# Output projections in column tiles that each run over all heads

## The chip, the cores and the metric

The kernel runs on one core of one Trainium2 chip. The metric is the device time of one execution in microseconds (us). Three runs of the kernel before took 823.28 to 824.87 us, with a median of 824.17 us.

## The reference

```
# A: attention over segments of 32 tokens with 8 recurrent memory tokens
xs_all = layernorm(x)                          # [2048, 512]
mem = mem0                                     # [8, 512]
for s in range(64):
    h = concat([mem, xs_all[32*s : 32*s+32]])  # 40 tokens
    q, k, v = h @ Wq, h @ Wk, h @ Wv           # 32 heads of 128
    scores = mask(q @ k.T * 128**-0.5)         # memory rows see all, token rows are causal
    o = softmax(scores) @ v
    o = sum over heads and e of o[t, h, e] * Wo[h, e, :]   # [40, 512]
    mem = o[:8]
    outs.append(o[8:])
h = x + concat(outs)
# B: a channel MLP
y = layernorm(layernorm(h))
out = h + gelu(y @ w1 + b1) @ w2 + b2
```

The inputs are bfloat16. The memory makes the segments a chain: a segment's first products need the first 8 rows of the output projection of the segment before. The change concerns the line with `Wo`.

## The kernel before

**Tiles and stages.** All four weight matrices stay in on-chip memory. Phase one is a loop over 64 segments; four segments make a block of 128 tokens. After it the MLP runs over four groups of 512 tokens. Tokens of a segment are held transposed in `hT` (feature by token, a ring of segments). A segment's 32 columns of `hT` are 24 token columns and 8 memory columns; the 8 remaining tokens of each segment are held in `hB`, one set for a block of four segments, and go through the projections a block ahead ("mixed-in" work, the parts named F).

**Column tiles.** Nearly all matmuls of phase one use TensorE in four column tiles of 32: a weight load puts 32 columns (the 32 tokens) into tile j, a matmul streams up to 512 columns of a weight matrix past it, and its 32 output rows land in partitions 32j to 32j+31 of a PSUM bank. Four matmuls, one for each tile, make a round and run at once.

**The order of work.** A small planner (`Sched`) records every operation with its reads and writes, and then lays out each engine's instruction stream. The order on TensorE is written out by hand (`ORDERS`, one for each position of a segment in its group of four): passes for Q, K and V, the memory scores SC0 and SC1, the products PV0, PV1 and PVA, the output projection WO, the self-attention scores SA, with the parts F0 and F1 in between. Other engines are placed by due times in a segment (`PLAN`). Parts F belong to the next block's Q, K and V in three of four segments; in the fourth (segment number 3 modulo 4), F1 is `wo_B`, the output projection of a block's mixed-in tokens.

**Instruction blocks.** TensorE's instructions are counted in blocks of 256 (`FETCH_N`). `align` counts each operation's instructions (`ni`) and inserts idle weight loads ("pads") into passes, at most 8 each, so that a segment's first instruction stands at a fixed place in its block (`PHASE`, by segment modulo 4). `windows` places DMA transfers from 1.0 us behind one block boundary to 0.8 us ahead of the next; `pauses` lets a few instructions behind a boundary wait for an earlier one of TensorE.

**The output projection.** `wo_units` (L1160 to L1173) makes eight units of eight matmuls, each 32 tokens by 256 columns over one head. Tiles 0 and 1 take half of the heads, tiles 2 and 3 the other half; of a pair, one takes the even 32-column groups of the output, the other the odd ones. So the sums over heads come in two halves, in the upper and the lower 64 partitions. In `wo` (L1178), VectorE transposes the 128x256 result in squares of 32 into `TT` (L1182), which makes it feature by token, and adds the halves (`halves_add`, L1176): first the 8 memory columns into the next segment's `hT`, by two additions of 64 partitions each, then the 24 token columns into `opT`, by two more. In three of four segments that second pair is kept back (`held`, `now`, `late`) and placed in the following segment, behind its softmax.

**The mixed-in projection.** `wo_B` (L1205) makes eight units of four matmuls with 512 columns. Each tile takes 8 of the 32 heads and all output columns, so four partial sums arise. VectorE transposes 128x512 into `TTB` (L1213). GpSimd folds them: `chunk` makes 7 operations for each half (L1222 to L1226), and `fold` spreads the 14 over the tails of three segments, each waiting for the one before.

**Behind it.** `nat` (L1238) turns `opT` back to rows by a DMA transpose, adds the residual, takes the layernorm's statistics in two halves of 256 columns (`half`, `close`; the second is kept back a segment) and stores the rows for the MLP.

Of the kernel before, what the change touches and what calls it, by code (L numbers as in the profile page):

```python
# [24 lines left out]
PHASE = (0, 64, 128, 192)  # L25
# [62 lines left out]
        "opA": (17.5, 10.96, 18.73, 17.5),  # L88
# [533 lines left out]
def build_kernel(nc, A_x, A_mem0, A_Wq, A_Wk, A_Wv, A_Wo, B_w1, B_b1, B_w2, B_b2, out):  # L622
# [3 lines left out]
    with st:  # L626
# [48 lines left out]
        TT = sb("TT", [P, 2, DC, 2, 32], F32)  # L675
        TTB = sb("TTB", [P, DC, 4, 32], F32)
        TTS = sb("TTS", [64, 2, 4, 32], F32)
# [4 lines left out]
        st2 = sb("st2", [P, 2, 2, 6], F32)  # L682
# [116 lines left out]
        turned, held, late, now = [], [], [], []  # L799
# [357 lines left out]
        def wo_cols(h, dh):  # L1157
            return WO[:, h, :].rearrange("p (b two e) -> p two b e", two=2, e=32)[:, dh]

        def wo_units(lhs, reads, bank):  # L1160

            for q in range(8):
                def f(e, q=q):
                    for k in (2 * q, 2 * q + 1):
                        for a in range(2):

                            h = (k // 8) * 16 + 8 * a + k % 8
                            for b in range(2):
                                j = 2 * a + b
                                ins = e.matmul(ps[bank][32 * j:32 * j + 32, 0:256], lhs(slot(h)), wo_cols(h, b), start=(k == 0), stop=(k == 15),  # L1170
                                               tile_position=(0, 32 * j), skip_group_check=True)
                    return ins
                S.op("pe", f, reads=[("WO", q, a) for a in range(2)] + reads(q // 4), writes=[("ps", bank)], dur=0.223, mode=MC, ni=16)  # L1173

        def halves_add(tt, q2, out, cols):
            return lambda e: e.tensor_tensor(out, tt[0:64, :, q2, cols], tt[64:128, :, q2, cols], ALU.add)  # L1176

        def wo(s, bank, mem=True, xrows=True):  # L1178
# [3 lines left out]
            S.op("dve", lambda e: e.transpose(tt.rearrange("p c q t -> p (c q t)"), ps[bank][:, 0:256]), reads=[("ps", bank)], writes=[("TT", par)], dur=t_dve(256) + 0.02)  # L1182
            if mem:
                sl = (s + 1) % RING
                S.op("dve", lambda e: [halves_add(tt, q2, hT[64 * q2:64 * q2 + 64, sl, :, NA:SEG], slice(NA, SEG))(e) for q2 in range(2)][1],
                     reads=[("TT", par)], writes=[("hTm", sl)], dur=0.4)
            if xrows:
                sx = s - 2
                o = opT[:, (sx // 4) % 2, :, 32 * (sx % 4):32 * (sx % 4) + NA]
                tag = S.tag  # L1190

                def rows(after=()):
                    was, S.tag = S.tag, tag
                    o_ = S.op("dve", lambda e: [halves_add(tt, q2, o[64 * q2:64 * q2 + 64], slice(0, NA))(e) for q2 in range(2)][1],
                         reads=[("TT", par)], writes=[("opA", (sx // 4) % 2, sx % 4)], dur=0.53, after=after)
                    S.tag = was
                    return o_
                if s % 4 == 2 and 1 < s // 4 < NTB - 3:
                    held.append(rows)
                elif s % 4 in (3, 0) and 3 < s < NS - 2:  # L1200
                    now.append(rows)
                else:
                    rows()

        def wo_B(bk, bank):  # L1205
            for q in range(8):
                def f(e, q=q):
                    for j in range(4):
                        ins = e.matmul(ps[bank][32 * j:32 * j + 32, :], OTB[:, bk % 2, slot(8 * j + q), :], WO[:, 8 * j + q, :], start=(q == 0), stop=(q == 7),  # L1209
                                       tile_position=(0, 32 * j), skip_group_check=True)  # L1210
                    return ins
                S.op("pe", f, reads=[("WO", g, a) for g in range(8) for a in range(2)] + [("OTB", bk % 2, sg) for sg in range(4)], writes=[("ps", bank)], dur=0.2135, mode=MC, ni=8)
            S.op("dve", lambda e: e.transpose(TTB[:].rearrange("p c q t -> p (c q t)"), ps[bank][:, :]), reads=[("ps", bank)], writes=["TTB"], dur=t_dve(512) + 0.02)  # L1213
            o = opT[:, bk % 2, :, :].rearrange("p c (s t) -> p c s t", s=4)[:, :, :, NA:SEG]

            def chunk(c):
                t = TTB[:, c:c + 2]

                def sums(q):
                    def f(e):  # L1220
                        x, y = [v[0:32, :, q].rearrange("p c (s t) -> p c s t", s=4) for v in (t, TTS)]
                        return e.tensor_tensor(o[32 * q:32 * q + 32, c:c + 2], x, y, ALU.add)  # L1222
                    return lambda after: S.op("pool", f, reads=["TTB", "TTS"], writes=[("opB", bk % 2)], dur=0.31, after=after)
                return [lambda after: S.op("pool", lambda e: e.tensor_copy(TTS[0:64], t[64:128]), reads=["TTB"], writes=["TTS"], dur=0.4, after=after),
# [6 lines left out]
        def fold(n, after=()):  # L1231
            tag, S.tag = S.tag, None
            for f in folds[:n]:
                S.narrow(f(after))
# [154 lines left out]
        for s in range(NS):  # L1389
# [7 lines left out]
            while held:  # L1397
                held.pop()()
# [288 lines left out]
```

## Time and profile before

| | |
|---|---|
| median of three runs | 824.17 us |
| profiled execution, its time | 821.98 us |
| its span, from the first to the last instruction | 820.2 us |
| granted TensorE clock, mean | 0.998 |
| WO matmuls (L1170) | 4224, 144.3 us busy |
| `wo_B` matmuls (L1209) | 512, 44.4 us busy |
| VectorE: transposes into `TT` and `TTB` | 29.1 and 11.3 us |
| VectorE: halves added into `hT` and `opT` | 24.7 and 33.5 us |
| GpSimd: folding (L1222 to L1226) | 40.3, 23.1, 12.6 and 12.4 us |

Busy times are those of one profiled execution. PE is TensorE's matmuls, PEld its weight loads, which overlap them; DVE is VectorE, ACT ScalarE, POOL GpSimd, SP the engine that issues most DMA transfers. The end of a matmul in the records is modelled and lies behind the start of the next one, so the time that a piece of work takes on TensorE is read from start to start. "issue" names idle time in which an engine waited for nothing that the profile shows.

### The profile page before, as it was taken

How to read it: one execution, taken by the hardware profiler on the slowest of the kernel's cores; microseconds unless marked ns; L12 is line 12 of the kernel's file. 1: busy time of each engine (PE TensorE's matmuls, PEld its weight loads, DVE VectorE, ACT ScalarE, POOL GpSimd, SP SyncE). 2: the span in 40 equal slices, each digit the busy share in tenths (PEclk: the TensorE clock that was granted, in tenths of full speed). 3: DMA queues.
4: the chain of work that ended last, by engine and by line, in shares of the span. 5: the costliest groups of instructions: out<-in, count | busy, mean ns of one | idle time of the engine just before them, and what ended most of it. 6: DMA issues, size and time to landing. Idle time of an engine off the chain costs nothing.

```text
span 820.2 us, 43608 instructions
## 1 busy us (share of the span) xinstructions
PE 783.0 (95%) x19317; PEld 425.6 (52%) x18878; DVE 620.3 (76%) x2022; ACT 534.5 (65%) x1512; POOL 350.3 (43%) x886
## 2 busy tenths in 40 slices
PE   3788999999999999999999999999999999999998
PEld 1355555555555555555555555555556555544443
DVE  3367898888888888888888888888889887833211
ACT  1546776767676767676777676767676768833442
POOL 5023333545454545454545444545463534267200
PEclk9999999999999999999999999999999999999999
DMA  8950010101011010101010101010112130265200
GB/s 341 390 174 12 4 33 7 33 27 29 29 27 33 20 39 17 42 13 45 10 43 10 48 11 49 11 48 3 50 29 61 40 96 17 75 165 137 72 26 26
DMA packets 65449, 48.03 MB, mean 59 GB/s; under 512 B 29028, under 2 KB 61676, under 8 KB 65260
## 3 DMA queue, kind: packets, MB, share of 16 engines
q1 hardware_dynamic: 64928, 44.98, 18.6%
q8 instruction: 150, 2.46, 1.3%
q14 instruction: 39, 0.32, 0.1%
q10 hardware_dynamic: 332, 0.27, 0.1%
HBM read 31.08 MB, written 8.13 MB: 48 GB/s over the span
## 4 chain that ended last, share of the span: by engine, by line
PE 74%; DVE 10%; ACT 8%; SPq 5%; issue 1%; DMA 1%; POOL 0%; DVEq 0%; POOLq 0%
PE ps L871 33%; PE ps L1170 14%; PE quad L1576 6%; PE ps L604 5%; PE ps L1569 4%; ACT EC L1053 4%; ACT kq L889 3%; PE quad L1074 3%; DVE PC L1061 3%; SPq L791 3%; DVE KALL L912 2%; SPq L774 2%; PE ps L1209 2%; PE ps L1104 2%; DVE nmc L1044 2%; PE quad L1142 1%
## 5 line engine op out<-in xcount | busy, mean ns | idle before, releaser
L871 PE MATMUL ps<-WQ,hT 128*32 128x512 bf16 x2048 | 157.9, 380 | 6.0 <-DVE hT L1176 5.5
L1170 PE MATMUL ps<-WO,OT 128*32 128x256 bf16 x4224 | 144.3, 275 | 1.3 <-issue 0.6
L871 PE MATMUL ps<-WV,hT 128*32 128x512 bf16 x1780 | 142.9, 379 | 0.0
L890 ACT ACTIVATE kq<-ps 128x512 bf16<-128x512 f32 x160 | 95.6, 598 | 62.1 <-PE ps L871 61.8
L1125 POOL TENSOR_TENSOR PA<-SA,rsa 128x256 bf16<-128x256 f32 x64 | 39.8, 621 | 189.3 <-DVE rsa L1118 176.8
L889 ACT CAST kq<-ps 128x512 bf16<-128x512 f32 x160 | 93.3, 583 | 36.6 <-PE ps L871 36.6
L1170 PEld LDWEIGHTS ps<-WO,OT 128*32 128x32 bf16 x4224 | 96.8, 96 | 26.6 <-ACT OT L889 5.2
L1131 POOL COPY BD<-PTA 32x192 bf16<-32x192 bf16 x256 | 96.1, 376 | 16.7 <-DVE PTA L1127 0.9
L871 PE MATMUL ps<-WK,hT 128*32 128x512 bf16 x1292 | 93.4, 379 | 0.0
L1061 DVE SCALAR_TENSOR_TENSOR PC<-EC,rsc,even 128x128 bf16<-128x128 f32 x256 | 87.9, 368 | 4.4
L871 PEld LDWEIGHTS ps<-WQ,hT 128*32 128x32 bf16 x2048 | 59.8, 96 | 59.9 <-issue 19.2
L912 DVE STREAM_TRANSPOSE KALL<-kq 128x256 f32<-128x256 f32 x160 | 70.5, 441 | 21.3 <-ACT kq L889 19.1
L1053 ACT ACTIVATE EC<-quad,nmc 128x64 f32<-128x64 f32 x252 | 77.2, 312 | 7.8 <-DVE nmc L1044 1.2
L604 PE MATMUL ps<-WK,hT 128*32 128x512 bf16 x756 | 75.7, 379 | 0.6 <-ACT kq L890 0.6
L889 ACT CAST VS<-ps 128x512 bf16<-128x512 f32 x126 | 73.8, 586 | 0.9
L871 PEld LDWEIGHTS ps<-WV,hT 128*32 128x32 bf16 x1780 | 52.0, 96 | 34.2 <-issue 2.0
L912 DVE STREAM_TRANSPOSE QT<-kq 128x256 f32<-128x256 f32 x128 | 56.8, 444 | 15.7 <-ACT kq L890 15.5
L889 ACT CAST OT<-quad 128x128 bf16<-128x128 f32 (+1 forms) x179 | 59.6, 348 | 11.4 <-PE quad L1079 8.3
L1572 ACT ACTIVATE WQ<-ps,b1t 128x512 bf16<-128x512 f32 x42 | 28.9, 688 | 51.9 <-PE ps L1569 51.9
L1116 ACT ACTIVATE SA<-SA 128x256 f32<-128x256 f32 x64 | 26.7, 417 | 55.1 <-DVE SA L1115 52.5
L871 PEld LDWEIGHTS ps<-WK,hT 128*32 128x32 bf16 x1292 | 38.1, 97 | 45.5 <-issue 20.3
L1222 POOL TENSOR_TENSOR opT<-TTB,TTS 32x64 bf16<-32x64 f32 x128 | 40.3, 315 | 33.2 <-DVE opT L1176 24.0
(160 smaller groups left out, 1487.6 us busy)
## 6 DMA issues: line engine op xcount, KB each, us to landing
WV<-in_A_Wv_dram SPq DMA_DIRECT2D x4, 1024.0 KB, 10.4
WK<-in_A_Wk_dram SPq DMA_DIRECT2D x4, 1024.0 KB, 18.0
WQ<-in_A_Wq_dram SPq DMA_DIRECT2D x4, 1024.0 KB, 19.1
WO<-in_A_Wo_dram SPq DMA_DIRECT2D x16, 256.0 KB, 7.5
v_last<-VSB SPq DMA_DIRECT2D x60, 64.0 KB, 3.2
VBD<-v_last SPq DMA_DIRECT2D x60, 64.0 KB, 2.8
h_mid<-xr SPq DMA_DIRECT2D x16, 128.0 KB, 1.8
WQ<-h_mid SPq DMA_DIRECT2D x4, 512.0 KB, 4.4
```

What stands on the lines that cost most here:

```text
L604: return e.add_instruction(mybir.InstMatmult(name="I-%d" % (4000000 + _kept[0]), engine=mybir.EngineType.PE, start_tensor_calc=start, stop ...
L871: ins = e.matmul(o, l, m, start=(k == 0), stop=(k == DC - 1), tile_position=(0, 32 * j), skip_group_check=True)
L889: return {"act": (lambda e: e.copy(out, src), t_act(n, ps_)), "dve": (lambda e: e.tensor_copy(out, src), 0.155 + 1.0e-3 * n * fast)}
L890: return {"act": (lambda e: e.mul(out, src, scale_), t_act(n, ps_)), "dve": (lambda e: e.tensor_scalar(out, src, scale_, None, ALU.mult), ...
L912: S.op("dve", lambda e: e.transpose(out, src), reads=[("kq", i)], writes=[key], dur=t_dve(256) + 0.02)
L1053: return e.activation(EC[:, r, sl, :], o[:, sl, :], ACTF.Exp, bias=nmc[:, r, sl:sl + 1], accum_out=smc[:, r, sl:sl + 1])
L1061: S.op("dve", lambda e, sl=sl, xc=xc: e.scalar_tensor_tensor(PC[:, r, :, :, sl], xc, rsc[:, r, sl:sl + 1], ev, ALU.mult, ALU.mult), reads= ...
L1125: S.either({k: ((lambda e: e.tensor_tensor(PA[:].rearrange("p a t b -> p a b t"), SA[:].rearrange("p (a b) t -> p a b t", b=2), bc2, ALU.m ...
L1131: S.narrow(S.op("pool", lambda e, j=j, rows=rows: e.tensor_copy(BD[rows, par, :, j, :, :], PTA[rows, :, 0:NA, :]), reads=["PTA"], writes=[ ...
L1170: ins = e.matmul(ps[bank][32 * j:32 * j + 32, 0:256], lhs(slot(h)), wo_cols(h, b), start=(k == 0), stop=(k == 15), tile_position=(0, 32 * ...
L1222: return e.tensor_tensor(o[32 * q:32 * q + 32, c:c + 2], x, y, ALU.add)
L1576: S.op("pe", lambda e: e.matmul(quad[:, t, :], gT_of(k, fc)[:, t * P:(t + 1) * P], W2[:, fc, :], start=(fc == 0), stop=(fc == FC - 1)), re ...
```

## The change

Each column tile j now takes the output columns 128c + 32j to 128c + 32j + 31 (c = 0 to 3) over all 32 heads, so that a projection is 128 matmuls of 128 columns, with a weight load each, and every sum is complete. The transposed result is 128x128 and needs plain copies instead of additions. `wo_B` uses the same units, and GpSimd's folding is gone. The copies into `opT` are no longer kept back; the statistics of `nat` are taken in one piece, and `nat` and the loads of x are issued a segment earlier. `PHASE`, the due times of `opA`, and the planner's durations are set anew.

```
-PHASE = (0, 64, 128, 192)
+PHASE = (216, 152, 152, 88)
...
-        "opA": (17.5, 10.96, 18.73, 17.5),
+        "opA": (19.07, 10.96, 10.96, 12.13),
...
-        def wo_cols(h, dh):
-            return WO[:, h, :].rearrange("p (b two e) -> p two b e", two=2, e=32)[:, dh]
+        def wo_cols(h, j):
+            return WO[:, h, :].rearrange("p (c j e) -> p j c e", j=4, e=32)[:, j]
...
             for q in range(8):
                 def f(e, q=q):
-                    for k in (2 * q, 2 * q + 1):
-                        for a in range(2):
-
-                            h = (k // 8) * 16 + 8 * a + k % 8
-                            for b in range(2):
-                                j = 2 * a + b
-                                ins = e.matmul(ps[bank][32 * j:32 * j + 32, 0:256], lhs(slot(h)), wo_cols(h, b), start=(k == 0), stop=(k == 15),
-                                               tile_position=(0, 32 * j), skip_group_check=True)
+                    for n in range(4):
+                        h = (q // 4) * 16 + 8 * (n // 2) + 2 * (q % 4) + n % 2
+                        for j in range(4):
+                            ins = e.matmul(ps[bank][32 * j:32 * j + 32, 0:P], lhs(slot(h)), wo_cols(h, j), start=(q == 0 and n == 0), stop=(q == 7 and n == 3),
+                                           tile_position=(0, 32 * j), skip_group_check=True)
                     return ins
-                S.op("pe", f, ..., dur=0.223, mode=MC, ni=16)
+                S.op("pe", f, ..., dur=0.2315, mode=MC, ni=32)
...
-            S.op("dve", lambda e: e.transpose(tt.rearrange("p c q t -> p (c q t)"), ps[bank][:, 0:256]), ...)
+            S.op("dve", lambda e: e.transpose(tt.rearrange("p c t -> p (c t)"), ps[bank][:, 0:P]), ...)
             if mem:
-                S.op("dve", lambda e: [halves_add(tt, q2, hT[64 * q2:64 * q2 + 64, sl, :, NA:SEG], slice(NA, SEG))(e) for q2 in range(2)][1], ...)
+                S.op("dve", lambda e: e.tensor_copy(hT[:, sl, :, NA:SEG], tt[:, :, NA:SEG]), ...)
             if xrows:
-                def rows(after=()): ...      # two halves_add into opT; held, now or at once
+                S.op("dve", lambda e: e.tensor_copy(o, tt[:, :, 0:NA]), ...)
...
         def wo_B(bk, bank):
-            for q in range(8): ...           # 4 matmuls of 512 columns, 8 heads for each tile
-            S.op("dve", lambda e: e.transpose(TTB[:].rearrange("p c q t -> p (c q t)"), ps[bank][:, :]), ...)
-            folds.extend(chunk(0) + chunk(2))
+            wo_units(lambda sl: OTB[:, bk % 2, sl, :], lambda r: [("OTB", bk % 2, sg) for sg in range(4)], bank)
+            S.op("dve", lambda e: e.transpose(TTB[:].rearrange("p c t -> p (c t)"), ps[bank][:, 0:P]), ...)
+            S.op("dve", lambda e: e.tensor_copy(o, TTB[:].rearrange("p c (s t) -> p c s t", s=4)), ...)
...
-            half(0)                          # bn_stats of 256 columns; close() does the second half later
+            S.op("dve", lambda e: e.bn_stats(st2[:, i, :], xs), ...)
...
-            if sg == 1 and 0 < bk and bk + 4 < NTB:
+            if sg == 0 and 0 < bk and bk + 4 < NTB:
                 load_x(bk + 4)
-            if sg == (3 if bk < NTB - 3 else 2) and bk > 1:
+            if sg == 2 and bk > 1:
                 nat(bk - 2)
```

More of the change, by code (lines that the diff above doesn't have):

```diff
@@ L797, in qbf @@
             return quad[:].bitcast(BF16)[:, :, 2 * c0:2 * c0 + P]
-        turned, held, late, now = [], [], [], []
+        turned = []
         def ln1(tb, after=()):
@@ L1198, in wo @@
[L1198 to L1203, printed above, removed]
-        def wo_B(bk, bank):
[L1206 to L1213, printed above, removed]
-            o = opT[:, bk % 2, :, :].rearrange("p c (s t) -> p c s t", s=4)[:, :, :, NA:SEG]
[L1216 to L1224, printed above, removed]
-                        lambda after: S.op("pool", lambda e: e.tensor_tensor(t[0:64], t[0:64], TTS[0:64], ALU.add), reads=["TTB", "TTS"], writes=["TTB"], dur=0.73, after=after),
-                        lambda after: S.op("pool", lambda e: e.tensor_copy(TTS[0:32], t[32:64]), reads=["TTB"], writes=["TTS"], dur=0.41, after=after)] + [sums(q) for q in range(4)]
-            folds.extend(chunk(0) + chunk(2))
```

62 lines of the change are left out of this document (15 added, 47 removed).

## The prediction

> **What bounds the kernel now.** I read the page first, for the engines' shares, the queues and the chain.
>
> ```profile
> span 820.2 us, 43608 instructions
> PE 783.0 (95%) x19317; PEld 425.6 (52%) x18878; DVE 620.3 (76%) x2022; ACT 534.5 (65%) x1512; POOL 350.3 (43%) x886
> ...
> q8 instruction: 150, 2.46, 1.3%
> ...
> PE 74%; DVE 10%; ACT 8%; SPq 5%; issue 1%; DMA 1%; POOL 0%; DVEq 0%; POOLq 0%
> ```
>
> TensorE is busy 95% and carries the chain, so GpSimd's 43% and VectorE's 76% are cover: relieving them pays only where TensorE waits for them. The row that I rest most on is the third (packets, MB, share of the DMA engines). TensorE's own instructions arrive in 150 packets: 2.46 MB / 150 is 16.4 KB each, and (19317 + 18878) / 150 is 255 instructions, so one packet is a block of 256 matmuls and weight loads (with a few separate waits). The change adds instructions to this queue and to nothing else. So I asked next, in the timeline of TensorE, what happens where a block ends. This is the second half of segment 20; columns are start, duration, engine, line, names, count:
>
> ```profile
> 256.92 0.41 PE L871 MATMUL ps<-WV,hT 128*32 128x512 bf16 x4
> 257.35 0.27 PE L1074 MATMUL quad<-PTC,VS 64*128 64x32 bf16 x8
> 257.46 0.23 PE L1079 MATMUL quad<-PTC,VBD 64*128 64x128 bf16 x2
> 257.66 0.38 PE L1142 MATMUL quad<-BD,VS 64*128 64x48 bf16 x16
> 257.97 0.40 PE L871 MATMUL ps<-WK,hB 128*32 128x512 bf16 x4
> 258.20 0.61 PE L1170 MATMUL ps<-WO,OT 128*32 128x256 bf16 x16
> 258.74 0.27 PE L1074 MATMUL quad<-PTC,VS 64*128 64x32 bf16 x8
> 258.85 0.22 PE L1079 MATMUL quad<-PTC,VBD 64*128 64x128 bf16 x2
> 259.00 1.53 PE L1170 MATMUL ps<-WO,OT 128*32 128x256 bf16 x48
> 260.35 0.39 PE L871 MATMUL ps<-WK,hB 128*32 128x512 bf16 x4
> 260.57 0.69 PE L1104 MATMUL ps<-KALL,QT 128*32 128x32 bf16 x32
> 261.08 0.83 PE L871 MATMUL ps<-WK,hB 128*32 128x512 bf16 x12
> ```
>
> The same self-attention scores (L1104, called SA in the code) in segment 24, and the weight loads of SA in segment 20:
>
> ```profile
> 302.53 0.42 PE L1104 MATMUL ps<-KALL,QT 128*32 128x32 bf16 x32
> 302.78 0.84 PE L871 MATMUL ps<-WK,hB 128*32 128x512 bf16 x12
> ```
>
> ```profile
> 260.36 0.36 PEld L1104 LDWEIGHTS ps<-KALL,QT 128*32 128x32 bf16 x13
> 260.96 0.19 PEld L1104 LDWEIGHTS ps<-KALL,QT 128*32 128x32 bf16 x19 [0.24 <-issue]
> ```
>
> SA took 0.51 us there (260.57 to 261.08) against 0.25 (302.53 to 302.78). The loads stop after 13 of 32 and nothing is waited for but "issue". By the code's count (`align`) a block of segment 20 begins two instructions into the V pass at 256.92 and ends inside SA. The rows agree: ahead of SA stand 4+8+2+16+4+16+8+2+48+4 = 112 matmuls, 224 instructions with their loads, 13 pairs of SA make 250, and the separate waits the rest. So TensorE stopped exactly where a block ended, 3.7 us after it began. The first segment shows it in the output projection itself:
>
> ```profile
> 58.73 1.38 PE L1170 MATMUL ps<-WO,OT 128*32 128x256 bf16 x42
> 60.70 0.40 PE L1170 MATMUL ps<-WO,OT 128*32 128x256 bf16 x6 [0.60 <-issue]
> ```
>
> 42 of 48 matmuls, then idle on "issue" at the next block's first instruction. I conclude that the next block is asked for when the present one is entered, and that a block run through faster than some time T stops TensorE until T is over. How often now, in the list of waits (us, times, longest):
>
> ```profile
> PEld L869 <- DVE hT L1176: 22.4, 48, 1.0
> PE ps L871 <- DVE hT L1176: 5.5, 7, 1.1
> PEld ps L1170 <- ACT OT L889: 5.2, 23, 0.3
> PEld ps L1104 <- issue: 2.2, 8, 0.4
> ```
>
> Eight stalls ahead of SA's loads; by the code's count one segment in four, fifteen in all, has a block that ends in SA when it is 3.7 us old. The kernel sits on the edge of T.
>
> **T, and its bounds.** The stalled SA had its block at about 3.7 + 0.3 = 4.0 us; the unstalled ones had it by 3.7. If eight of fifteen took 4.0 and the other seven as little as 2.5, the mean is 3.3; if those took 3.7, 3.9. Below, no row excludes a smaller T, since a fetch that is not late leaves no row; I keep 2.8 as the low end (one in which seven of fifteen needed 1.4). I take T = 3.3, the low side, because the code keeps its own transfers away from the first 1.0 us after a block boundary (`windows`), and short blocks leave no room for one behind it that could delay the fetch.
>
> **The change, part by part.** *Instructions.* An output projection goes from 64 to 128 matmuls, each with its load: +128 instructions in each of 66. The mixed-in projection `wo_B` goes from 32 to 128 matmuls: +192 in each of 16. So 4x128 + 192 = 704 more per four segments, and `PHASE` says the same: the segments' starting places 0, 64, 128, 192 close after 9 blocks of 256, the new ones 216, 152, 152, 88 after 12 (with some 64 idle loads as padding).
>
> *Where the blocks end.* Counted in instructions from a segment's start, the new layout has the first two projection units at 330 to 394, the second PV at 394 to 414, the six other units to 606, then SA to 670. Boundaries lie at 256k minus the segment's phase. Times between them come from the rows of segment 20 (two units 0.54, PV 0.26, six units 1.35):
> - phase 216: at 40, 296 (in PVA, L1142) and 552 (fifth of the six units): 257.7 to 259.0 + 4.3 x 0.225 = 2.3 us;
> - phase 152, twice: at 104, 360 (end of the first unit) and 616 (in SA): 0.27 + 0.26 + 1.35 + 0.05, about 2.0 us each;
> - phase 88, where the passes between are `wo_B` units of 32 instructions: at 168, 424 (start of the projection), 680 (sixth of six) and 40 of the next segment: about 2.8, 0.54 + 0.26 + 5.4 x 0.225 = 2.0, and 2.7 us.
>
> The six other blocks of a group hold mostly passes of 8 instructions in 0.215 us and last 4.1 to 5.3 us. The six short ones together last 13.8 us and would need 6T: at T = 3.3 that is 19.8, so 6.0 us lost per four segments. Segments 4 to 63 are 15 groups: **+90 us**. At T = 2.8 the block of 2.8 drops out, 5 x 2.8 - 11.0 = 3.0, +45; at 3.85, 9.3 and +140. The opening segments and the tail, with half as many such blocks: +4 (2 to 6).
>
> *The matmuls themselves.* Rounds of four column tiles, from starts: 16 matmuls of 64 columns with 16 loads took 0.12 us, 0.030 a round; twelve rounds of 256 columns 1.35, 0.112.
>
> ```profile
> 401.49 0.30 PE L1036 MATMUL quad<-KALL,ZC 128*32 128x64 bf16 x16
> 401.61 0.39 PE L871 MATMUL ps<-WV,hT 128*32 128x512 bf16 x4
> ```
>
> Between them 128 columns take 0.057: 32 x 0.057 = 1.83 against 16 x 0.112 = 1.79 for a projection, 1.83 against 8 x 0.215 = 1.72 for `wo_B`. 66 x 0.04 + 16 x 0.11 = 4.4, taken as **+5** (0, if columns alone count, to 8).
>
> The Trainium skill, "TensorE: Matmul & The Clock Gate", section "LDWEIGHTS (loading the stationary operand)", speaks against the change: a load takes its columns / 1.2 ns, 27 ns for 32 columns, 107 ns for a round's four against some 55 of matmul. The 0.030 us round above holds four such loads, so this trace disagrees unless the four column tiles load at once.
>
> *The memory chain.* After the projection VectorE transposes, adds halves twice, and only then can the next segment's first pass load hT.
>
> ```profile
> L1182 DVE STREAM_TRANSPOSE TT<-ps 128x256 f32<-128x256 f32 x66 | 29.1, 440 | 26.9 <-PE ps L1170 26.8
> L1176 DVE TENSOR_TENSOR hT<-TT 64x32 bf16<-64x32 f32 x126 | 24.7, 196 | 3.0
> L1063 DVE STREAM_TRANSPOSE PTC<-PC 128x128 f32<-128x128 f32 x128 | 39.9, 311 | 4.4
> L1176 DVE TENSOR_TENSOR opT<-TT 64x96 bf16<-64x96 f32 x128 | 33.5, 262 | 2.9
> L1222 POOL TENSOR_TENSOR opT<-TTB,TTS 32x64 bf16<-32x64 f32 x128 | 40.3, 315 | 33.2 <-DVE opT L1176 24.0
> L1225 POOL TENSOR_TENSOR TTB<-TTB,TTS 64x256 f32<-64x256 f32 x32 | 23.1, 721 | 15.7 <-DVE PC L1061 14.0
> ```
>
> 440 + 2 x 196 = 832 ns becomes 311 (the 128x128 transpose) plus one copy of about 190: 0.33 us shorter. What that was worth:
>
> ```profile
> 408.39 0.41 PE L871 MATMUL ps<-WQ,hT 128*32 128x512 bf16 x4
> ...
> 417.98 0.84 PE L1209 MATMUL ps<-WO,OTB 128*32 128x512 bf16 x12
> 418.85 0.41 PE L871 MATMUL ps<-WQ,hT 128*32 128x512 bf16 x4
> ```
>
> Three rounds of 0.215 end at 418.63, the pass starts at 418.85: 0.22 us lost in a segment of 10.46. Over 63 segments that is 14 at most; the 48 waits of weight loads for hT (22.4 us, in the list above) are mostly hidden behind running matmuls, so I take 7. The 2.2 us of SA stalls and some of the 5.2 for OT fall under the new stalls too. Together **-12** (-5 to -16).
>
> *The rest costs nothing on the path.* The row copies (two adds of 262 ns become one), the smaller transpose in `wo_B`, and GpSimd's folding (40.3 + 23.1 us and the copies beside them) lie on engines with idle time. `nat` (a DMA transpose, then a 128 KB store) and `load_x` (a 128 KB load) move a segment earlier in SP's queue, past that segment's other transfers; none of TensorE's waits listed above is for SP. Undivided statistics hold VectorE about 0.26 us longer at a stretch, 16 times: 4 us if none of it were covered, and the stops of TensorE now cover it.
>
> **Sum**, against the profiled execution: 821.98 + 90 + 4 + 5 - 12 = 909. The median of the runs stands 0.27% above the profiled one, so **911**.
>
> **Rivals.** *A: blocks are never late, and the gains stand.* Then 822 + 5 - 12 + (the OT waits that stay) 3 = 818, with the median's 0.27% 820, a gain of 0.5%. For it: at 3.7 us only half of the SA stalled. Against it: two stops exactly at a block's end, one in the projection. It decides if T is below about 2.0. The Trainium skill, "Runtime: NRT & Kernel Launch", section "Instruction fetch mechanics", gives PE room for 2048 instructions, which would make every block early, and says in the same place that the next page is fetched while the current one runs; the stops bear out the second. I give A 0.11, and 0.03 that small stops (T near 2.1) and gains cancel to within 0.2%, which is about what a measurement of this kernel can tell from no change.
>
> *B: weight loads bound the projection*, one after another. With 0.0275 us per load, the most that hides under today's 0.11 us round of four, a round takes 0.11 instead of 0.057: 32 x 0.053 x 82 = +139, on top of A less its 5, some 954, without any idle "issue" row. SA's and L1036's rows, with loads in 0.008 us each, are against it: 0.02. By the 27 ns of the page of the Trainium skill named above it would be 950.
>
> *C: T is small but not harmless*, 2.1 to 2.8: 826 to 866. For it: the low end above is not excluded. 0.14.
>
> My forecast, T between 2.8 and 3.9, has the rest, 0.70; by itself it spans 860 to 966. Range 826 to 966: the low end takes in C, so that A, the balance near zero and B stay out (0.16), the high end is T = 3.85 with the dear ends of the small terms. Faster 0.11, same 0.03, slower 0.86.
>
> **What would show it.** Queue q8 has about 197 packets, and PE x25,077. Rows L1170's successor and L1104 gain idle "<-issue" of about 1 to 1.5 us, in all four kinds of segment, at the places above; segments last about 11.5 to 13 us, the one with `wo_B` longest. The wait of L871 for hT vanishes. A projection whose matmuls run 1.8 us without an "issue" gap, with hT's wait gone, would prove me wrong and A right; even slow rounds without gaps, B.

## The result: slower by 12.8%, and the profile after

| | before | after |
|---|---|---|
| median of the runs | 823.72 us (822.25 to 824.87, 4 runs) | 928.92 us (926.93 to 930.52, 4 runs) |
| profiled execution, time and span | 821.98 and 820.2 us | 927.4 and 925.7 us |
| granted TensorE clock, mean | 0.998 | 0.996 |

The ratio is 1.128, with a 95% interval from 1.124 to 1.131. The clock is the same, so the 105 us are not a slower TensorE.

The page of after, with the lines that answer to the first ones shown of before (span, engines, the queue of TensorE's instructions, the chain), and its groups of the projection and of the self-attention scores (SA):

```profile
span 925.7 us, 55633 instructions
PE 794.1 (86%) x25068; PEld 469.3 (51%) x25558; DVE 571.7 (62%) x1912; ACT 528.1 (57%) x1497; POOL 261.7 (28%) x662
...
q8 instruction: 199, 3.26, 1.5%
...
PE 70%; issue 11%; ACT 8%; DVE 6%; DMA 2%; SPq 2%; POOL 0%; DVEq 0%
...
L1166 PE MATMUL ps<-WO,OT 128*32 128x128 bf16 x8448 | 152.7, 221 | 42.6 <-issue 38.9
...
L1103 PE MATMUL ps<-KALL,QT 128*32 128x32 bf16 x2048 | 31.4, 178 | 41.7 <-issue 41.7
```

Every engine but TensorE has less to do: VectorE is down from 620.3 to 571.7 us, GpSimd from 350.3 to 261.7. TensorE is busy 11 us more, at 86% instead of 95%, and the chain has 11% "issue", where it had 1%: 11% of 925.7 is 102 us. Almost all of the loss is TensorE standing still and waiting for nothing that the profile shows. The list of waits (us, times, longest) says where:

```profile
PE ps L1103 <- issue: 41.7, 32, 2.0
PE ps L1166 <- issue: 38.9, 34, 2.1
PE ps L870 <- issue: 15.9, 17, 3.2
```

41.7 + 38.9 + 15.9 = 96.5 us. The waits for hT are nearly gone: of the 22.4 us for which TensorE's loads waited for it before, 5.6 are left, in two rows:

```profile
PEld ps L870 <- DVE hT L1178: 4.6, 14, 0.3
...
PEld L868 <- DVE hT L1178: 1.0, 2, 0.5
```

Where the stops stand, in TensorE's timeline: all stops on "issue" from segment 15's end to segment 19's, and one row (277.50) in which a wait is put down to ScalarE.

```profile
232.61 0.34 PE L1166 MATMUL ps<-WO,OT 128*32 128x128 bf16 x10 [1.77 <-issue]
...
236.07 0.40 PE L870 MATMUL ps<-WQ,hT 128*32 128x512 bf16 x4 [0.69 <-issue]
...
245.04 0.57 PE L1166 MATMUL ps<-WO,OT 128*32 128x128 bf16 x28 [1.16 <-issue]
...
257.06 0.35 PE L1103 MATMUL ps<-KALL,QT 128*32 128x32 bf16 x26 [1.07 <-issue]
...
268.97 0.34 PE L1103 MATMUL ps<-KALL,QT 128*32 128x32 bf16 x26 [1.48 <-issue]
...
277.50 0.63 PE L1166 MATMUL ps<-WO,OT 128*32 128x128 bf16 x32 [0.33 <-ACT OT L888]
...
280.96 0.34 PE L1166 MATMUL ps<-WO,OT 128*32 128x128 bf16 x10 [1.23 <-issue]
```

These are the boundaries of the prediction: ahead of the last pass of Q0 and in the fifth of six projection units (phase 216), in SA (phase 152, twice), at the start of the projection and in its sixth unit (phase 88). The resumed rows hold what is left of the pass: 26 of SA's 32 matmuls. TensorE's records show the blocks exactly: each of these rows begins 256 records, or 512 or 768, behind another. So does the row at 277.50. In 14 groups, TensorE began there between 0.36 us ahead of the end of ScalarE's operation and 0.69 us behind it, so that operation isn't what releases it: this is the sixth stop, 0.4 us in the mean.

The fetches themselves are in the trace too, as packets of q8. From 254 to 260 us, around the stop of 257.06, they are the only two transfers (busy tenths of the DMA engines in 40 slices of 0.15 us, and the queue's packets):

```profile
DMA  0000400000000000000000000004000000000000
...
q8 instruction: 2, 0.03, 2.2%
```

The block that ends in this stop was entered at 253.80, 256 records ahead of the resume. The next block's packet starts at 254.75 and takes 0.96 us; TensorE resumes 1.35 us after it has landed. From 80 to 770 us every block has exactly one such packet. In the mean of the six stopped places (14 groups), it starts 1.04 us behind the block's first instruction and takes 1.11 us, and TensorE goes on 1.38 us after its end: 3.53 us from a block's first instruction to the next one's. A block that TensorE runs through in less time ends in a stop.

And the projection itself, in the second of these segments, ahead of the stop in SA:

```profile
254.44 1.52 PE L1166 MATMUL ps<-WO,OT 128*32 128x128 bf16 x96
255.79 0.21 PE L1103 MATMUL ps<-KALL,QT 128*32 128x32 bf16 x6
```

Six units with twice the matmuls and loads take 255.79 - 254.44 = 1.35 us, just what they took before (259.00 to 260.35 in the prediction's rows). Here the new form isn't slower; it is run through just as fast, and then its next block isn't there.

How much a group of four segments takes, from the start of the first pass of segment 4 to that of segment 60, in before and then in after:

```profile
82.97 0.41 PE L871 MATMUL ps<-WQ,hT 128*32 128x512 bf16 x4 [0.78 <-DVE hT L1176]
...
670.80 0.41 PE L871 MATMUL ps<-WQ,hT 128*32 128x512 bf16 x4
```

```profile
89.06 0.40 PE L870 MATMUL ps<-WQ,hT 128*32 128x512 bf16 x4 [0.41 <-DVE hT L1178]
...
766.90 0.40 PE L870 MATMUL ps<-WQ,hT 128*32 128x512 bf16 x4
```

(670.80 - 82.97) / 14 = 41.99 us before, (766.90 - 89.06) / 14 = 48.42 us after: 6.43 us for every four segments. This group time is the measure in the experiments below; it leaves out the opening and the tail, and it is read from the profiled execution alone.

### The profile page after: what moved, and what is told of

It reads as the page before. It is cut to its first block, busy times and chain, and to the rows that moved or that the text cites. A ratio compares the mean times of both kernels' runs of the same rounds, so it can differ in the third digit from the quotient of the medians.

```text
span 925.7 us, 55633 instructions
## 1 busy us (share of the span) xinstructions
PE 794.1 (86%) x25068; PEld 469.3 (51%) x25558; DVE 571.7 (62%) x1912; ACT 528.1 (57%) x1497; POOL 261.7 (28%) x662
## 4 chain that ended last, share of the span: by engine, by line
PE 70%; issue 11%; ACT 8%; DVE 6%; DMA 2%; SPq 2%; POOL 0%; DVEq 0%
PE ps L870 30%; PE ps L1166 17%; PE ps L604 5%; PE quad L1509 5%; PE ps L1502 4%; ACT EC L1052 3%; PE quad L1073 3%; ACT kq L888 3%; PE ps L1103 2%; DMA WQ<-in_A_Wq_dram 2%; DVE KALL L911 2%; DVE PC L1060 2%; SPq L773 2%; PE ps L1307 1%; DVE nmc L1043 1%
## 5 line engine op out<-in xcount | busy, mean ns | idle before, releaser
L1166 PE MATMUL ps<-WO,OT 128*32 128x128 bf16 x8448 | 152.7, 221 | 42.6 <-issue 38.9
L870 PE MATMUL ps<-WQ,hT 128*32 128x512 bf16 x2048 | 160.6, 380 | 14.0 <-issue 12.3
L1166 PEld LDWEIGHTS ps<-WO,OT 128*32 128x32 bf16 x8448 | 122.6, 97 | 65.4 <-issue 45.9
L889 ACT ACTIVATE kq<-ps 128x512 bf16<-128x512 f32 x146 | 87.2, 597 | 115.7 <-PE ps L870 115.5
L870 PE MATMUL ps<-WV,hT 128*32 128x512 bf16 x1780 | 143.0, 379 | 0.0
L870 PEld LDWEIGHTS ps<-WQ,hT 128*32 128x32 bf16 x2048 | 59.8, 96 | 71.6 <-issue 27.2
L870 PE MATMUL ps<-WK,hT 128*32 128x512 bf16 x1292 | 93.3, 379 | 0.3 <-issue 0.3
L1175 DVE STREAM_TRANSPOSE TT<-ps 128x128 f32<-128x128 f32 x66 | 20.9, 317 | 98.2 <-PE ps L1166 98.2
L888 ACT CAST OT<-quad 128x128 bf16<-128x128 f32 (+1 forms) x206 | 65.7, 354 | 13.6 <-PE quad L1078 11.8
L1103 PE MATMUL ps<-KALL,QT 128*32 128x32 bf16 x2048 | 31.4, 178 | 41.7 <-issue 41.7
L870 PEld LDWEIGHTS ps<-WV,hT 128*32 128x32 bf16 x1780 | 51.8, 96 | 30.1 <-issue 1.6
```

What stands on the lines that cost most here:

```text
L870: ins = e.matmul(o, l, m, start=(k == 0), stop=(k == DC - 1), tile_position=(0, 32 * j), skip_group_check=True)
L888: return {"act": (lambda e: e.copy(out, src), t_act(n, ps_)), "dve": (lambda e: e.tensor_copy(out, src), 0.155 + 1.0e-3 * n * fast)}
L889: return {"act": (lambda e: e.mul(out, src, scale_), t_act(n, ps_)), "dve": (lambda e: e.tensor_scalar(out, src, scale_, None, ALU.mult), ...
L1103: ins = e.matmul(ps[bank][32 * j:32 * j + 32, 32 * k:32 * k + 32], QT[:, h // 2, :, h % 2], KALL[:, par * HP + h // 2, :, h % 2], start=Fa ...
L1166: ins = e.matmul(ps[bank][32 * j:32 * j + 32, 0:P], lhs(slot(h)), wo_cols(h, j), start=(q == 0 and n == 0), stop=(q == 7 and n == 3), tile ...
```

## The experiments

Theory F is the prediction's: a block of 256 instructions is fetched while the block before it runs, that takes over 3 us, and the added instructions make blocks that run through in 2. The rivals: the 128-column matmuls themselves (M), the steps moved across segments (P), an unlucky place of the boundaries (K), and other transfers that slow the fetch (D).

| kernel | median, us | ratio to before, 95% | group of four, us |
|---|---|---|---|
| before / after | 823.72 / 928.92 | 1.124 to 1.131 | 41.99 / 48.42 |
| old projection, idle loads added | 930.56 | 1.126 to 1.136 | 49.15 |
| new projection, loads left out | 824.88 | 1.000 to 1.003 | 41.78 |
| after, moved steps put back | 933.09 | 1.130 to 1.134 | 48.64 |
| after, two F passes among the WO units | 927.08 | 1.122 to 1.127 | 48.23 |
| only the segments' projection | 914.65 | 1.108 to 1.113 | 47.40 |
| only `wo_B` | 845.48 | 1.025 to 1.029 | 43.25 |
| after, boundaries shifted | 947.64 | 1.145 to 1.157 | 49.56 |
| after, transfers kept farther away | 935.28 | 1.131 to 1.138 | 48.61 |
| before, one burst of idle loads | 859.43 | 1.041 to 1.045 | |
| before, SA two passes later | 822.27 | 0.997 to 0.999 | 41.91 |

The profiled execution of the kernel with idle loads added was the longest of its four (937.99 us), so its group time is rather long.

### The instructions without the projection

The kernel before, with idle weight loads beside the old matmuls, so that every pass has the change's number of instructions:

```
-PHASE = (0, 64, 128, 192)
+PHASE = (216, 152, 152, 88)
...
 # wo_units, ahead of each of the 64 matmuls (and 6 ahead of each of wo_B's 32)
+    for _ in range(2):
+        e.ldweights(lhs(slot(h)), tile_position=(0, 32 * j))
```

> The kernel before, with idle weight loads beside those of the output projections, so that TensorE has exactly as many instructions in exactly the places of the kernel after (PHASE as there); the 64 matmuls of 256 columns, the additions of halves, GpSimd's folding and every other step stay as before. If the instruction blocks are the cause, it takes as long as after or a little longer, since the longer memory chain stays: 925 to 940 us. If the 128-column matmuls are (rival M), or the moved and undivided steps (rival P), it stays near 824 us.

930.56 us: all of the loss, with no matmul changed, and VectorE and GpSimd still adding and folding. The page and the waits:

```profile
PE 808.7 (86%) x19308; PEld 475.5 (51%) x31318; DVE 626.3 (67%) x2022; ACT 533.4 (57%) x1512; POOL 348.7 (37%) x886
...
q8 instruction: 199, 3.26, 1.5%
```

```profile
PE ps L1104 <- issue: 41.3, 32, 1.9
PE ps L1172 <- issue: 39.5, 33, 1.8
PE ps L871 <- issue: 10.1, 15, 1.0
```

The same 199 packets, and the same stops in the same passes (41.3 for SA, 39.5 in the projection) as after. M is out: no matmul was changed (19,308 are on the page, 19,317 on that of before).

### The projection without the instructions

The other way round: the 128 matmuls of 128 columns and the new evacuation, but about as many instructions as before.

```
 # wo_units of the segments: a load only ahead of the first round of units 0 and 2
+    if kept and not (q in (0, 2) and n == 0):
+        ins = matmul_kept(e, o, l, m, ...)       # no weight load
 # wo_B: the old 32 matmuls, loads mostly left out; PHASE of before
```

> The kernel after, with the weight loads of the output projections left out except at the first matmuls behind a change of mode (so the products are of stale weights), and the mixed-in projection's matmuls as before with most loads left out; PHASE as before. TensorE has as many instructions as before in about the places of before, but 128 matmuls of 128 columns for a segment, and all other steps as after. If the instruction blocks are the cause: 812 to 824 us, below before if the shorter memory chain pays. If 128-column matmuls themselves are slow (M) or the moved steps (P): it stays near 929 us.

824.88 us, 0.03% to 0.29% above before: the loss is gone, and so is the gain that had been expected of the shorter memory chain. Matmuls, queue and waits:

```profile
PE 780.0 (95%) x23532; PEld 351.5 (43%) x15150; DVE 573.1 (70%) x1926; ACT 524.2 (64%) x1483; POOL 260.6 (32%) x662
...
q8 instruction: 152, 2.49, 1.3%
```

```profile
PE ps L1103 <- issue: 3.4, 10, 0.6
PE ps L870 <- issue: 3.0, 1, 3.0
```

A group lasts 41.78 us, 0.21 less than before, about 3 us over the kernel. Taken pass by pass, from start to start, those at the segments' ends, behind which the waits for hT lay, are 0.43 us a group shorter; SA (0.16) and the projection's units (0.12) are longer. The stop in the opening (3.0 us) takes the rest back. Together the two kernels say that the count of instructions makes the loss, and that the better form of the projection is worth next to nothing here.

### The moved steps

```
-            if sg == 0 and 0 < bk and bk + 4 < NTB:
+            if sg == 1 and 0 < bk and bk + 4 < NTB:
                 load_x(bk + 4)
-            if sg == 2 and bk > 1:
+            if sg == (3 if bk < NTB - 3 else 2) and bk > 1:
                 nat(bk - 2)
```

> The kernel after, with the loads of x and the turning back to rows (load_x, nat) issued in the segments of before. Instruction blocks: no change, 925 to 933 us. Rival P (the moved steps collide with transfers on SP's queue, and delay the fetches or the softmax): 20 us or more faster.

933.09 us. Putting them back gains nothing; if anything it costs 0.4%. The undivided statistics and the copies at once stay in this kernel, but they are in the one with loads left out as well, which is as fast as before. P is out.

### Long passes among the projection's units

If a block needs a time from its beginning, and not a fixed stop, passes of few instructions put into the dense stretch should shorten the stop. In three kinds of segment:

```
-('WO', 2, 8), ('F1', 3, 4), ('SA', 0, 99), ('F0', 1, 4)
+('WO', 2, 4), ('F1', 3, 4), ('WO', 4, 6), ('F0', 1, 2), ('WO', 6, 8), ('SA', 0, 99), ('F0', 2, 4)
```

> The kernel after, with two passes of the mixed-in work moved from behind SA (or ahead of it) into the six projection units in three of four kinds of segment; same instructions, same count. A block that runs from the projection into SA holds two passes of 0.215 us more and so is older by 0.2 to 0.43 us when it ends. If blocks have to last a time T, its stop shrinks by as much: 3 x 0.2 to 0.43 x 15 = 9 to 19 us, less what the thinner cover of the memory chain costs (up to 0.2 us in those segments, 9 us): 910 to 929 us. If a block end costs a fixed stop whatever its age, or if matmuls are slow (M): 929 to 940 us.

927.08 us, and 48.23 for 48.42 in a group: inside what was expected, at its weak end, and with an interval that overlaps that of after, so the time alone decides nothing. The second kind of segment, ahead of its stop:

```profile
257.02 0.61 PE L1166 MATMUL ps<-WO,OT 128*32 128x128 bf16 x30
258.31 0.23 PE L1166 MATMUL ps<-WO,OT 128*32 128x128 bf16 x2 [0.68 <-issue]
```

```profile
PE ps L1166 <- issue: 50.2, 50, 1.5
PE ps L870 <- issue: 28.6, 30, 2.9
PE ps L1103 <- issue: 5.8, 4, 1.9
```

The stop has left SA (5.8 us instead of 41.7) and become shorter where a long pass went in ahead of it, 0.68 here against 1.07. In the mean of 14 groups, start to start, the three stops went from 1.20, 1.50 and 1.42 us to 1.04, 1.06 and 1.18, while their blocks kept their length (3.60, 3.52 and 3.44 us in after, 3.46, 3.42 and 3.54 here). That is a time, not a fixed stop. (L870's row grew because the first of the three now resumes in one of the moved passes; no new stop came up.) But a stopped block lasts its 3.5 us whatever is in it. A group can only gain what the blocks behind lose, and they lost little, 4.06 to 3.95 us and 5.04 to 4.90.

### One half of the change, and the other

Only the segments' projection (8,192 instructions more in 64 segments), with `wo_B` and its folding as before:

```
-PHASE = (0, 64, 128, 192)
+PHASE = (0, 192, 128, 64)
...
 # wo_units as in the change for the segments; wo_B, chunk and fold as before
```

> Only the segments' projection of the change (8 passes of 16 pairs, rows copied, not folded); branch B's small projection and its folding as before; 11 instruction blocks per four segments, 183 in all (before 145-150, after 192-199). Theory F (a block of 256 instructions can't follow the one before by less than about 3.2 us): by the places of the blocks and the passes' own times, four of the eleven are short (those ending at Q0 of the first kind, at the last WO of the first and second kind and at SA of the third: 2.3, 2.7, 2.2, 1.8 us), 3.8 to 4.3 us lost per four segments, none in the fourth kind: +60 to +67 us, less up to 8 from the waits that go, 875 to 893 us. Rival M (a matmul of 128 columns is dearer by itself): 64 x 8 x (0.223-0.218) = +3 us, 827 us, with the time spread evenly over all WO passes. Rival P (the steps moved across segments, load_x and nat): 824 us, since nothing of that is in it.

And only `wo_B`:

```
 # wo_B: 8 units of 16 matmuls of 128 columns; TTB copied to opT, no chunk, no fold; the rest as before
```

> Only branch B's projection of the change (two passes of 32 pairs instead of 16, copies instead of folding); the segments' projection as before; 10 blocks per four segments, 166 in all. Theory F: at 3.2 to 3.3 us a block, two of the ten are short (at Q0 of the first kind, 2.3 us, and at the pass after wo_B in the fourth kind, 3.1 us): 1.05 to 1.25 us per four segments, +16 to +19 us, 838 to 844 us. Rival in proportion to the instructions (every added one costs the same 105 us / 11,968): +33 us or more. Rival M or P: 824 us, nothing.

`wo_B` alone: 845.48 us, a little above the 838 to 844 expected, and +1.26 us for a group where 1.05 to 1.25 was. That is well below the 33 us or more that a cost in proportion to the instructions would give (21.8 us). Most of it is the stop expected at Q0, some 1 us a group:

```profile
PEld L869 <- issue: 17.7, 15, 1.6
```

The other short block, the one behind `wo_B`, wasn't stopped; SA of the first kind was instead, by 0.2 us more than before. The segments' projection alone: 914.65 us, above the 875 to 893 expected. Its group is 47.40, +5.4 where 3.8 to 4.3 was expected. The four places foretold stop, and with them a fifth that the expectation had ruled out, the last WO units of the fourth kind (0.7 us):

```profile
PE ps L1167 <- issue: 39.0, 45, 1.5
PE ps L871 <- issue: 20.4, 16, 3.3
PE ps L1104 <- issue: 18.0, 15, 1.8
```

The stop at Q0 (most of the second row) is the one behind this fifth stop, and its block lasted 3.76 us in the mean of 14, not 3.2. Of the three whose block began without a stop two lasted 3.33 and 3.30 us, the third, in the first kind, 4.22: there the fetch started only 1.73 us behind the block's first instruction.

### Other places for the boundaries

```
-PHASE = (216, 152, 152, 88)
+PHASE = (88, 24, 24, 216)
```

> The changed kernel with the instruction places shifted by padding loads, so that the block boundaries fall about half a block later in each kind of segment; nothing else differs. Theory F: 12 blocks per four segments whatever their places, and short ones remain: 4.4 to 5.1 us lost per four segments instead of 5.6 to 6.2, 908 to 918 us; the stops leave SA for F0, F1, Q0 and the last WO passes. Rival K (only an unlucky place of the boundaries): most of the 105 us gone, 830 to 860 us.

947.64 us: slower by 2%, where both theories expected faster. K is out, the change's own places were among the better ones; the working with one time of 3.2 to 3.3 us for all blocks is out too. Here stops come in pairs, one right behind the other. Two such pairs, from the third kind of segment into the fourth and inside the fourth:

```profile
270.71 1.01 PE L1166 MATMUL ps<-WO,OT 128*32 128x128 bf16 x58 [1.43 <-issue]
274.45 0.40 PE L870 MATMUL ps<-WQ,hT 128*32 128x512 bf16 x4 [0.30 <-issue]
...
282.01 1.24 PE L1166 MATMUL ps<-WO,OT 128*32 128x128 bf16 x74 [0.52 <-issue]
285.75 0.79 PE L1166 MATMUL ps<-WO,OTB 128*32 128x128 bf16 x42 [1.92 <-issue]
```

274.45 - 270.71 and 285.75 - 282.01 are 3.74 us both. That suggested that a stream of short blocks has a slower rate than one short block behind a long one, and the burst below measures it. But after has such pairs too. What is dearer here is the block that ends at the first row, 270.71: it lasted 4.74 us in the mean of 13 (4.58 to 4.88), because its fetch started 2.29 us behind its first instruction; the packet took 1.10 us, as elsewhere. At 3.5 us it would make the group 1.2 us shorter, and the group is only 1.14 longer than after's.

### Transfers away from the boundaries

```
-WINDOWS, WIN_LO, WIN_HI = True, 1.0, -0.8
+WINDOWS, WIN_LO, WIN_HI = True, 2.0, -0.8
```

> The changed kernel with the issue of its own transfers kept 2.0 us, not 0.4, behind a block boundary, so that fewer of them share the DMA engines with the fetch of a block. Rival D (other transfers delay the fetch, and so set its 3.2 us): time from resume to resume of a stopped block falls to about 2.9 us, six short blocks per four segments gain 0.3 us each, down to 900 us. Theory F without D (the fetch takes this long by itself): 924 to 932 us, resume to resume still 3.1 to 3.3 us. Later transfers can make a wait of their own: then slower, with waits on DMA in the profile.

935.28 us, not faster, and a little above the 924 to 932 that F gave; a group lasts 48.61. (The expectation's "0.4" was a slip: the distance was 1.0 us before.) The blocks that end in SA lasted 3.37 and 3.48 us in the two kinds of segment (3.52 and 3.44 after). The distance is the planner's, whose times hold no stops, so transfers still fall beside fetches. The traces decide it all the same: of 80 stopped blocks of after, 23 have no other transfer from their first instruction to the resume, and they last 3.42 us, with 1.11 us for the fetch; those with a transfer beside the fetch last 3.57. In this kernel 35 of 80 have none, and last 3.53. D is worth 0.1 to 0.2 us a block in the segments, and the rest of the 3.5 is the fetch's own. The opening is another matter, below.

### The price of a block by itself

The kernel before, with 2,560 idle loads at one place, ten blocks, so that nothing else changes its place in its block:

```
 # wo_units, segment 33
+    if burst and q == 4:
+        for n in range(2560):
+            e.ldweights(lhs(slot(16)), tile_position=(0, 32 * (n % 4)))
```

> The kernel before with one burst of 2,560 idle weight loads (ten instruction blocks, the places of everything else in its block unchanged) ahead of the fifth projection pass of segment 33: the price of a block by itself, with nine short blocks in a row and hardly a transfer beside them. Theory F with one time for every block: stops every 256 loads, resume to resume 3.1 to 3.2 us each, burst 30 to 31 us, about 854 us. Theory F with a slower rate where short blocks follow one another (what the last round hints at: 3.6 us at stops that follow a stop, 3.1 us at others): first 3.1, then 3.5 to 3.7 us each, burst 34 to 36 us, about 858 us. Rival (loads cost their issue alone, about 8 ns each, no stops): 20 us, 844 us.

859.43 us, 35.7 more than before. The weight loads in the burst, in the timeline:

```profile
396.37 1.42 PEld L1166 LDWEIGHTS <-OT 128*32 128x32 bf16 x292 [0.22 <-ACT OT L889]
399.84 1.79 PEld L1166 LDWEIGHTS <-OT 128*32 128x32 bf16 x256 [2.05 <-issue]
403.31 1.79 PEld L1166 LDWEIGHTS <-OT 128*32 128x32 bf16 x256 [1.69 <-issue]
406.79 1.78 PEld L1166 LDWEIGHTS <-OT 128*32 128x32 bf16 x256 [1.68 <-issue]
410.53 1.79 PEld L1166 LDWEIGHTS <-OT 128*32 128x32 bf16 x256 [1.96 <-issue]
...
432.45 0.56 PEld L1173 LDWEIGHTS ps<-WO,OT 128*32 128x32 bf16 x14 [1.51 <-issue]
```

This is the clearest picture of the mechanism. The first row runs on over a boundary that came early in it: 292 loads are 36 and a whole block. From there, every row is a block of 256, run through in about 1.7 us and followed by a stop. The starts of the rows are 3.47 or 3.74 us apart, and (432.45 - 399.84) / 9 = 3.62 in the mean. The first block took about 3.3 (36 loads of some 5 ns behind 396.37, to 399.84). So the short block behind a long one had its successor after 3.3 us, and the row of short blocks behind it goes at 3.62 each: the second of the three cases that the expectation gave. The difference lies in the fetch's start. It comes 0.90 us behind the first instruction of the first block and 1.13 us, in the mean, behind those of the nine others. In after it is less marked: blocks that begin without a stop last 3.4 to 3.6 us by place, those that begin with one 3.6.

### A version that is faster than both

The block at which the kernel before stops in its segments ends in SA of the first kind. Two small passes ahead of SA make it longer:

```
-('WO', 2, 8), ('F1', 3, 4), ('SA', 0, 99), ('F0', 1, 4)
+('WO', 2, 8), ('F1', 3, 4), ('F0', 1, 3), ('SA', 0, 99), ('F0', 3, 4)
```

> The kernel before with the sums of the scores' rows (SA) two small passes later in the first kind of segment, the only block of before that is at the edge (ends in SA about 3.6 us after it began, with stops of 0.17 us in the mean, 15 times): the block becomes about 4.05 us. Theory F: those stops go, up to 15 x 0.17 = 2.6 us, 821 to 823 us against 823.7, ratio 0.997 to 0.999; less if what follows SA now waits for it. Rival (SA's idle time there has another cause than the block): 823.7 us or slower.

822.27 us in 12 runs against 823.75 in 17, ratio 0.9978 (0.9969 to 0.9987): faster than before, by the amount expected, though hardly more than can be measured. SA of segment 20 runs through:

```profile
261.26 0.82 PE L871 MATMUL ps<-WK,hB 128*32 128x512 bf16 x12
261.90 0.42 PE L1104 MATMUL ps<-KALL,QT 128*32 128x32 bf16 x32
262.15 0.41 PE L871 MATMUL ps<-WK,hB 128*32 128x512 bf16 x4
```

0.25 us from start to start, where the prediction's row had 0.51, and SA's loads no longer appear among the waits for "issue" (2.2 us in 8 before).

## Why the prediction was right, step by step

**The mechanism** held at each sign that the prediction named: 199 packets (some 197 foretold) and 25,068 matmuls (25,077); "issue" ahead of SA and in the projection, in all four kinds of segment, at the boundaries worked out; segments of 12.1 us in the mean. One sign was off: the longest segment is not the one with `wo_B` (12.31 us) but the one behind it (12.66), in which that block's stop at Q0 falls. The two kernels that separate the instructions from the projection show it as the cause: each has one half of the change, and only the one with the instructions is slow.

**The stops, +90.** This is the term that was too small. The time of a block T was taken as 3.3 us from a single stalled place, with bounds of 2.8 and 3.9. The six stopped blocks of after lasted 3.4 to 3.6 us by place, 3.53 in the mean. The value was near, and in part by luck: it was the mean of 4.0 us at the stalled place and a guess of 2.5 where there was no stop. By the fetches of before, that place needed 4.05 us in the mean: 1.59 to the fetch's start, 1.08 for the packet, and the 1.38 of after from there to the resume. A T of its own for each place is what the prediction didn't have. The stops add up to 7.1 us in a group (each stopped pass against its undisturbed fellows: 6.7 for the five on "issue", 0.4 for the sixth) where 6T - 13.8 = 6.0 was foretold. The difference, 1.1 x 15 = 16 us, is what this term lacked.

**Opening and tail, +4.** Mis-sized: segment 1's first pass starts 3.0 us later than before (at 53.84, not 50.87), and the part behind segment 63's start is 4.9 us longer (120.2, not 115.3), 7.9 in all. Most of the opening is one stop:

```profile
48.30 1.04 PE L870 MATMUL ps<-WQ,hB 128*32 128x512 bf16 x8 [3.23 <-issue]
```

It falls into the time in which the weight matrices are loaded. The busy tenths of the DMA engines from 45.0 to 48.5 us, in 40 slices:

```profile
DMA  9999999999999999999999999998765555578499
```

The fetch of this stop starts at 45.92 us, 4.0 us behind its block's first instruction (41.96), where 1.04 is the mean of the stopped places in the segments; the packet then takes 1.16 us, hardly more than elsewhere. Late is its start, among the other transfers. That they make it late is likely, but wasn't tried. In the kernel before a fetch starts as late (46.55, 3.9 us behind 42.67), but the block there lasts longer still. The kernel with few loads has a stop of 3.0 us there as well with about as many instructions as before, so it is a matter of where a boundary falls. In the tail, after's chain holds 2.81 us of waiting for a weight of the MLP (WK from B's w1); what brings that about wasn't tried.

**The matmuls, +5.** Where no stop or wait falls into them, six units went from 1.32 to 1.35 us, 0.005 a unit: 0.005 x 8 x 66 = 2.6 us, and `wo_B` (0.68 us for three units, not 0.645) adds 1.5. The term was about right. The 27 ns for a load, which the Trainium skill gives in "TensorE: Matmul & The Clock Gate", section "LDWEIGHTS (loading the stationary operand)", are not borne out as a price paid for each load in turn: 96 loads and 96 matmuls took 1.35 us, 14 ns a pair. What one load takes while those of the other three column tiles run, the rows don't tell.

**The waits that go, -12.** Rounds and waits together come to 6.43 - 7.1 = -0.7 us a group, -10 us, where the prediction had 5 - 12 = -7. What the passes show of it: SA of the first kind lost its old stop (0.16 us a group), and the passes ahead of the next segment's start, in which the waits for hT lay, are 0.10 and 0.14 us shorter in the second and third kind; in the fourth the sixth stop hides it (0.21 in the kernel with loads left out). So the gain was there, and the stops outweighed it ten times.

So the sum came to 911 where 928.92 was measured: the stops 16 us too small, opening and tail 4, and rounds and waits 3 better than foretold.

**The rivals.** A (never late) and B (loads in a row) are refuted by the rows above; the room for 2,048 instructions that the Trainium skill states ("Runtime: NRT & Kernel Launch", section "Instruction fetch mechanics") would have let 2,560 idle loads stop TensorE late and seldom; it stopped at every 256 of them from the second block on. C (T of 2.1 to 2.8) is below what the burst shows. A slip in the prediction changes none of this: it says that B stays out of its range, but B's 954 us lies inside 826 to 966.

**What stays open.** Why a fetch starts 0.9 us behind its block's first instruction at one place and 2.3 at another, as in the kernel with shifted boundaries; that start, not the packet's time, makes most of the difference between places. And why the times in the burst are 3.47 or 3.74 and nothing between: at one place in after, the start of the projection, the blocks lasted 2.99, 3.2, 3.49, 3.76 or 4.04 us, steps of some 0.27 as well. No experiment explains these.

## What to carry to other kernels

Count a change's instructions, not only its columns: where a TensorE pass is run through faster than its instructions arrive (here 256 in some 3.5 us, 14 ns each), an added load or matmul can cost its share of a fetch, and work taken off other engines didn't pay for it here. Look for "issue" rows with a fixed number of instructions between them and for the instruction queue's packets, and see by an experiment with idle loads whether the count alone makes the loss. If one block is at the edge, move passes of few instructions ahead of its end; where six of twelve were, that gained next to nothing.

## What the runs showed of the hardware beyond that

- In after, each block of 256 instructions has one packet of the instruction queue. At the stopped places it starts 1.04 us behind the block's first instruction, takes 1.11 us, and TensorE goes on 1.38 us after its end (1.19 to 1.59): 3.53 us in the mean of 14 groups.
- The packet's time hardly differs (1.10 us in the kernel with shifted boundaries' dearest place, 1.16 in the opening, where the DMA engines were nine tenths busy), its start does: 2.29 us there, 4.0 in the opening.
- A row of short blocks goes at 3.62 us for 256 instructions (3.47 or 3.74 each); the short block ahead of that row lasted 3.3.
- Of 80 stopped blocks of after, the 23 with no other transfer beside them lasted 3.42 us, those with one beside the fetch 3.57.
- Idle weight loads of 32 columns ran at 256 in about 1.7 us, below 7 ns each, while nothing else stood in the way.
